# A recurrent attention block with a feed-forward layer: the output product regrouped into four 160-column strips, and the memory rows turned by VectorE instead of TensorE

## The chip, the cores and the metric

The kernel runs on one core of a Trainium2 chip. Its time is the device time of one execution in microseconds (us). Before the change three runs gave a median of 1040.74 us (1040.04 to 1044.46). The engines are TensorE (PE in the profile; its weight loads are shown as PEld), VectorE (DVE), ScalarE (ACT), GpSimd (POOL) and the queue that issues most DMAs (SP).

## The reference

An input of 2048 tokens with 640 channels goes through two layers: `h = x + A(layernorm(x))`, then `h + B(layernorm(h))`. A is attention with 32 heads of 128, computed in 64 segments of 32 tokens, one after the other, because each segment hands 8 memory rows to the next:

```python
mem = mem0                                    # 8 rows of 640
for s in range(64):
    h = concat([mem, x[32*s : 32*s+32]])      # 40 rows
    q, k, v = h @ Wq, h @ Wk, h @ Wv          # 32 heads x 128
    p = softmax(mask(q @ k.T * scale))
    o = (p @ v) @ Wo                          # 40 rows of 640
    mem = o[:8]                               # the next segment needs it
    outs.append(o[8:])
```

B is a feed-forward layer of width 1728 with a squared ReLU. Inputs and outputs are bf16.

## The kernel before

**Stages.** A start-up stage loads the weights and projects the first segment. Then 64 calls of `step` (L368) do one segment each, some 12.9 us apart. At the end the feed-forward layer runs in four tiles of 512 tokens (L780 on).

**What a step does.** The 40 rows of a segment are split: 8 memory rows and the first 24 tokens (the main rows, 32 in all) are handled in the step; the last 8 tokens of four segments are collected to 32 tail rows for whole-block products. TensorE is used in four column groups of 32: four matmuls with weights of 128x32 run side by side and write partitions 0-31, 32-63, 64-95 and 96-127 of one PSUM tile. In this text such four are a round, and a weight load with its matmul is a pair.

The order on TensorE in a step, which is written out by hand and is kept by every engine as written: the projections q, k, q, k from `hT` (`proj`, L194; each 20 pairs of 512 columns), the memory rows' scores, the values' projection v, the scores of the segment's tokens, the attention values of the segment before (`token_values`, L336) and of the memory rows (`values`, L431), then the output product of all 32 heads into the PSUM tile `pw` (`wo_rounds`, L229, called at L542).

**The output product before.** For 16 rounds, the column groups are two halves of the heads (kh) times two halves of the 640 output columns (ch), 320 columns each. So `pw` holds two partial sums in its upper and lower 64 partitions, and `wo_out` (L239) adds them: ScalarE copies the lower half to `otmp` (L243), VectorE adds the upper half to it and writes `o` (L244). The tail rows' product (`wo_tail_units`, L285) works the same way, once for four segments.

**The memory rows' way to the next segment.** `mem_to_hT` (L304) takes `o`, transposes its first rows on TensorE by 20 small matmuls against an identity (L308, tile `pm`), and VectorE copies the result into `hT` (L310), from which the next step's projections read.

**Fill work.** Products that no step waits for are cut into units and put in a list, `fill`: projections of tail rows (units of 4 pairs of 512 columns) or the tail rows' output product (10 units). A step takes one unit at L509, two at L520, five between `wo_out` and `mem_to_hT` (L549) and what is left at L553. `tails_in` (L312) copies the tail rows' q and k into place on GpSimd, and `token_out` (L351) moves attention values on ScalarE and GpSimd. `store_main` (L328) issues the DMAs of finished rows from SP. Five `o` tiles form a ring (`o_ring`).

Of the kernel before, what the change touches and what calls it, by code (L numbers as in the profile page):

```python
# [9 lines left out]
ALU = mybir.AluOpType  # L10
AX = mybir.AxisListType
F32 = mybir.dt.float32
BF16 = mybir.dt.bfloat16
# [3 lines left out]
def kernel(  # L17
# [16 lines left out]
    nc = tc.nc  # L34
    _, S, D = A_x.shape
    _, H, E = A_Wq.shape
    M = A_mem0.shape[1]
    SEG = 32
# [3 lines left out]
    EG = HE // G  # L42
    DC = D // 128
    DH = D // 2
    NB = S // 128
    NS = S // SEG
    HD = 24
# [13 lines left out]
    const = ctx.enter_context(tc.tile_pool(name="const", bufs=1))  # L61
# [6 lines left out]
    s1 = ctx.enter_context(tc.tile_pool(name="s1", bufs=1))  # L68
    s2 = ctx.enter_context(tc.tile_pool(name="s2", bufs=2))

    o_all = dram.tile([S, D], BF16)
# [4 lines left out]
    wo = wts.tile([128, H, D], BF16)  # L76

    ident = const.tile([128, 128], BF16)
# [13 lines left out]
    for g in range(G):  # L92
        r = slice(32 * g, 32 * g + 32)
# [6 lines left out]
    oT = const.tile([128, H, NK], BF16)  # L100
    nc.vector.memset(oT[:], 0.0)
    oTts = [const.tile([128, H, 32], BF16, name="oTt%d" % k) for k in range(2)]
# [3 lines left out]
    def head(p):  # L106

        n, g, j = p // 16, p // 4 % 4, p % 4
        return g * HG + j * 2 + n
# [16 lines left out]
        eng.dma_start(out=xt[:], in_=x2d.rearrange("(s t) d -> s t d", t=SEG)[16 * g:16 * g + 16, HD:SEG, :])  # L126
        xts["t", g] = xt

    o_ring = [const.tile([128, DH], BF16, name="o%d" % k) for k in range(5)]
    for o in o_ring:  # L130
        nc.gpsimd.memset(o[64:128], 0.0)
    o0 = o_ring[-1]
    nc.vector.memset(o0[0:64], 0.0)
    load_x(0)
    for ch in range(2):
        nc.sync.dma_start(out=o0[32 * ch:32 * ch + M, :].rearrange("m (c f) -> m c f", f=64),
                            in_=A_mem0[0].rearrange("m (c t f) -> t m c f", t=2, f=64)[ch])
    load_tail_rows(0)
    load_w(wv, A_Wv)
    def load_wo():  # L140
# [19 lines left out]
    hT4s, hTts, tails = {}, {}, {}  # L160
# [63 lines left out]
    def flip(row, dst, n):  # L224
        nc.vector.transpose(out=dst[:, n * 16:(n + 1) * 16, 0:32], in_=row.rearrange("p (h e) -> p h e", e=32))  # L225

    wov2 = wo[:].rearrange("p h (c t f) -> p h t c f", t=2, f=64)

    def wo_rounds(lhs, pw, h0, h1):  # L229

        for h in range(h0, h1):
            for kh in range(2):
                for ch in range(2):
                    j = kh * 2 + ch
                    p = h // 8 * 16 + kh * 8 + h % 8
                    nc.tensor.matmul(pw[32 * j:32 * j + 32, 0:DH], lhsT=lhs(p), rhs=wov2[:, head(p), ch],  # L236
                                     start=(h == 0), stop=(h == 15))

    def wo_out(pw):  # L239
        o = o_ring[0]  # L240
        o_ring.append(o_ring.pop(0))
        tmp = s1.tile([128, DH], F32, tag="tk", name="otmp")
        nc.scalar.copy(out=tmp[0:64], in_=pw[64:128, 0:DH])  # L243
        nc.vector.tensor_tensor(out=o[0:64], in0=pw[0:64, 0:DH], in1=tmp[0:64], op=ALU.add)  # L244
        return o

    fill, late, mid, win = [], [], [], []

    def run(q, n):
        while n > 0 and q:  # L250
            q.pop(0)()
            n -= 1
# [32 lines left out]
    def wo_tail_units(b):  # L285
        st = {}

        def out():
            o = wo_out(st["ps"])
            dst = o_all[:].rearrange("(b s t) d -> b s t d", s=4, t=SEG)  # L290
            for ch in range(2):
                nc.sync.dma_start(out=dst[b, :, HD:SEG, ch * DH:(ch + 1) * DH], in_=o[32 * ch:32 * ch + 32, :])

        def unit(k):
            def f():
                if k == 0:
                    st["ps"] = mmtile()
                wo_rounds(lambda p: oTts[b % 2][:, p, :], st["ps"], k * 16 // 10, (k + 1) * 16 // 10)
                if k == 9:
                    late.append(out)  # L300
            return f
        return [unit(k) for k in range(10)]

    def mem_to_hT(o, hT4, sp):  # L304
        pm = chn.tile([128, 512], F32, tag="ch", name="pm")
        for c in range(DC):
            for q in range(4):
                nc.tensor.matmul(pm[32 * q:32 * q + 32, c * M:(c + 1) * M], lhsT=o[:, (2 * c + q % 2) * 32:(2 * c + q % 2 + 1) * 32],  # L308
                                 rhs=ident[:, q // 2 * 32:q // 2 * 32 + M], start=True, stop=True)
        nc.vector.tensor_copy(out=hT4[:, :, sp, 0:M], in_=pm[:, 0:DC * M].rearrange("p (c m) -> p c m", m=M))  # L310

    def tails_in(b, sp):  # L312
        q, k = [tails[b][w][:].rearrange("p h (k s) -> p h s k", s=4)[:, :, sp, :] for w in "qk"]
        nc.gpsimd.tensor_copy(out=qT[:, :, SEG:NK], in_=q)
        nc.gpsimd.tensor_copy(out=kT[:, :, SEG:2 * SEG].rearrange("p h (j k) -> p h j k", k=TL),  # L315
                              in_=k.unsqueeze(2).to_broadcast([128, H, 4, TL]))
# [9 lines left out]
            eng.dma_start(out=vt4s[b][32 * g:32 * g + 32].rearrange("p s u e -> p (s u e)"), in_=src[g])  # L326

    def store_main(o, s):  # L328
        for ch in range(2):
            nc.sync.dma_start(out=o_all[s * SEG:s * SEG + HD, ch * DH:(ch + 1) * DH],  # L330
                              in_=o[32 * ch + M:32 * ch + 32, :])

    oTg = oT[:].rearrange("p (n g j) q -> p n g j q", n=2, g=G)
    back = []
# [33 lines left out]
    def step(b, sp, v=None):  # L368
        s = b * 4 + sp
        last = s == NS - 1  # L370
        hT4 = hT4s[b]
        lhs = lambda c: hT4[:, c, sp, :]
# [151 lines left out]
        tk = s1.tile([128, HG, NK], F32, tag="tk", name="tk")  # L524
# [3 lines left out]
        for f in outs:  # L528
# [7 lines left out]
                                op=ALU.mult)  # L536
        pk = s1.tile([128, HG, 32], BF16, tag="pk", name="pk")
        nc.gpsimd.tensor_tensor(out=pk[:], in0=ek[:, :, 0:SEG], in1=rk[:].unsqueeze(2).to_broadcast([128, HG, SEG]),
                                op=ALU.mult)

        pw = chn.tile([128, 512], F32, tag="ch", name="pw")
        wo_rounds(lambda p: oT[:, p, 0:32], pw, 0, 16)  # L542
        o = wo_out(pw)
        if s:
            token_out(s - 1, po)
        if s > 1:
            store_main(o, s - 2)
        if not last:
            run(fill, 5)  # L549
            mem_to_hT(o, hT4s[(s + 1) // 4], (s + 1) % 4)  # L550
            tails_in((s + 1) // 4, (s + 1) % 4)
        run(mid, 2)
        run(fill, 100)  # L553
        pTt = s1.tile([128, 2, 32], BF16, tag="pTt", name="pTt")
# [2 lines left out]
        for u in range(2):  # L557
            nc.gpsimd.tensor_tensor(out=pTx[:, u], in0=pTt[:, u, HD:32].unsqueeze(1).to_broadcast([128, 4, TL]),
                                    in1=same[:], op=ALU.mult)
# [60 lines left out]

    def prep_sum(t, k, got):
        ot, fx = got
        fv = fx.rearrange("p (c t f) -> p t c f", t=2, f=64)
        nc.vector.tensor_tensor(out=fv, in0=ot.rearrange("p (t c f) -> p t c f", t=2, f=64), in1=fv, op=ALU.add)
        return fx

    def prep_norm(t, k, ht, mv, rs):
# [75 lines left out]
    load_w(wq, A_Wq)  # L703
    ln_stats(("t", 0))
    ln_transpose(0)()
    mem_to_hT(o0, hT4s[0], 0)
    ln_norm(("t", 0))
    load_x(1)
    load_w(wk, A_Wk)
# [50 lines left out]

    def end_output(s):
        pw = chn.tile([128, 512], F32, tag="ch", name="pw")
        wo_rounds(lambda p: oT[:, p, 0:32], pw, 0, 16)
        store_main(wo_out(pw), s)

    def end_tails():
# [13 lines left out]
    for t in range(S // NT):  # L780
# [6 lines left out]
        for fc in range(FC):  # L787
            ps = mmtile()
            for c in range(DC):
                if fc < FFULL:  # L790
                    nc.tensor.matmul(ps[:], lhsT=w1[:, c, fc * 128:(fc + 1) * 128], rhs=hnT[:, c, :],  # L791
                                     start=(c == 0), stop=(c == DC - 1))
                    continue
                for hh in range(2):
                    nc.tensor.matmul(ps[FREM * hh:FREM * (hh + 1), 0:HT], lhsT=w1[:, c, fc * 128:F],
                                     rhs=hnT[:, c, HT * hh:HT * (hh + 1)], start=(c == 0), stop=(c == DC - 1))
            w = NT if fc < FFULL else HT
            r = rs_[fc % 4]
            nc.scalar.activation(out=r[:, 0:w], in_=ps[:, 0:w], func=ACT.Relu, bias=b1f[:, fc:fc + 1], scale=1.0)
            nc.vector.tensor_tensor(out=f1T[:, fc, 0:w], in0=r[:, 0:w], in1=r[:, 0:w], op=ALU.mult)  # L800
            if more and fc >= 1 and (fc - 1) // 3 < NK4:
                k, stage = divmod(fc - 1, 3)
# [10 lines left out]
        for q in range(NK4):  # L813
# [6 lines left out]
            for hh in range(2):  # L820
                k = pr + 2 * hh
                for fc in range(FFULL):
                    nc.tensor.matmul(y[:, hh, 0:DH], lhsT=f1T[:, fc, k * 128:(k + 1) * 128], rhs=w2[:, fc, cs],  # L823
                                     start=(fc == 0), stop=False, skip_group_check=True)
                if more and q and (hh == 0 or q == 1):
                    k = q if hh == 0 and q > 1 else hh
# [45 lines left out]
```

## Time and profile before

| what | value |
|---|---|
| median of three runs | 1040.74 us |
| span of the profiled execution, first to last instruction | 1035.5 us |
| from the first to the last step's output product | 66.1 to 881.9 us |
| TensorE busy, pairs | 980.1 us (95%), 26960 |
| VectorE, ScalarE, GpSimd busy | 621.6, 536.0, 312.3 us |
| output product of the main rows (L236, `pw`) | 4224 pairs of 320 columns, 159.6 us |
| output product of the tail rows (L236, `ps`) | 1024 pairs of 320 columns, 47.0 us |
| transposes of the memory rows (L308) | 1280 pairs of 8 columns, 18.6 us |
| granted TensorE clock, mean | 0.993 |

The profiled execution has no total of its own beside its span; the median of the runs lies 5.2 us above the span, which is what lies around it. [...] In the timeline each line gives the start, the length, the engine, the line of code, what is written and read, the shape and the number of merged instructions; in brackets stands how long the engine sat idle before and what ended it. The profile's third part lists DMA queues; the queue called instruction carries the program's own instructions to an engine.

### The profile page before, as it was taken

The page shows a single profiled execution, that of the slowest core. Times are in us where ns is not written, and L with a number is a line of the kernel's source. Part 1 is how long each engine was busy: PE and PEld are TensorE (multiplying, and loading weights), DVE is VectorE, ACT ScalarE, POOL GpSimd, SP SyncE. Part 2 cuts the span into 40 slices and gives each one's busy share as a digit, 9 for nine tenths or more (in the row PEclk, how much of TensorE's full clock was granted, in tenths as well). Part 3 has the DMA queues.
Part 4 walks back from the last instruction along what each step waited for, and adds up shares of the span by engine and source line. Part 5 has one row for each costly group of instructions (what it writes and reads, how often), then busy time and mean ns, then how long its engine had stood idle before and what let it go on. Part 6 is the DMA issues. An engine that isn't in the chain of part 4 may idle for free.

```text
span 1035.5 us, 58905 instructions
## 1 busy us (share of the span) xinstructions
PE 980.1 (95%) x26960; PEld 563.9 (54%) x26960; DVE 621.6 (60%) x1740; ACT 536.0 (52%) x1225; POOL 312.3 (30%) x805
## 2 busy tenths in 40 slices
PE   5879899999999999999999999999999998999998
PEld 2335455555655555555555655555555555555565
DVE  2155666766566666666666666666666676565432
ACT  2435555555555555555555555555555555534431
POOL 1033333333333333332333233333333333343210
PEclk9889999999999999999999999999999999999999
DMA  8960101000100000000000000000000110612200
GB/s 319 405 205 26 22 7 31 7 24 6 32 10 22 15 24 24 16 20 14 26 15 22 15 27 15 22 15 27 15 21 8 47 33 7 194 54 72 77 26 26
DMA packets 39112, 51.58 MB, mean 50 GB/s; under 512 B 6160, under 2 KB 34960, under 8 KB 36944
## 3 DMA queue, kind: packets, MB, share of 16 engines
q1 hardware_dynamic: 38000, 47.30, 13.8%
q8 instruction: 210, 3.44, 1.4%
q14 instruction: 38, 0.31, 0.1%
q10 hardware_dynamic: 544, 0.26, 0.1%
q0 software_dynamic: 320, 0.26, 0.1%
HBM read 38.37 MB, written 9.44 MB: 46 GB/s over the span
## 4 chain that ended last, share of the span: by engine, by line
PE 83%; DMA 6%; DVE 5%; issue 3%; ACT 2%; POOL 0%; SPq 0%; DVEq 0%; ACTq 0%; POOLq 0%
PE ps L204 45%; PE pw L236 13%; PE y L823 6%; PE ps L791 5%; PE ps L236 3%; DMA xt<-in_A_x_dram 3%; PE po L437 2%; PE pm L308 2%; PE sm L409 2%; DMA wq<-in_B_w_dram 1%; PE po L343 1%; PE ps L485 1%; ACT em L418 1%; DMA vt_d<-row 1%; DVE o L244 1%
## 5 line engine op out<-in xcount | busy, mean ns | idle before, releaser
L204 PEld LDWEIGHTS <-hT 128*32 128x32 bf16 x7680 | 186.9, 96 | 180.8 <-DVE hT L310 19.6
L204 PE MATMUL ps<-wv,hT 128*32 128x512 bf16 x2520 | 169.9, 379 | 0.7 <-ACT v L492 0.7
L236 PE MATMUL pw<-wo,oT 128*32 128x320 bf16 x4224 | 159.6, 300 | 3.3 <-DVE pTt L555 1.2
L204 PE MATMUL ps<-wq,hT 128*32 128x512 bf16 x2520 | 158.1, 380 | 4.8 <-DVE hT L310 4.8
L204 PE MATMUL ps<-wk,hT 128*32 128x512 bf16 x2520 | 157.6, 379 | 0.0
L236 PEld LDWEIGHTS <-oT 128*32 128x32 bf16 x4224 | 109.3, 97 | 50.7 <-DVE oT L211 15.8
L535 POOL TENSOR_TENSOR pkt<-ek,rk 128x64 bf16<-128x64 bf16 x64 | 18.8, 294 | 377.6 <-DVE rk L533 377.6
L220 ACT ACTIVATE row<-ps 128x512 bf16<-128x512 f32 x156 | 91.9, 601 | 78.4 <-PE ps L204 74.6
L225 DVE STREAM_TRANSPOSE qT<-row 128x512 bf16<-128x512 bf16 x128 | 90.6, 709 | 51.9 <-ACT row L220 51.9
L222 ACT CAST row<-ps 128x512 bf16<-128x512 f32 x115 | 65.9, 596 | 34.3 <-PE ps L204 34.3
L315 POOL COPY kT<-kTt 128x1024 bf16<-128x1024 bf16 x64 | 70.9, 1108 | 13.7 <-DVE kTt L225 13.7
L362 POOL COPY qz<-qT 128x96 bf16<-128x96 bf16 x126 | 33.4, 265 | 125.0 <-DVE qT L225 121.5
L353 ACT CAST oT<-po 128x512 bf16<-128x512 f32 x128 | 68.7, 589 | 1.6
L244 DVE TENSOR_TENSOR o<-pw,otmp 64x320 bf16<-64x320 f32 x66 | 31.8, 482 | 61.9 <-ACT otmp L243 61.9
L204 PEld LDWEIGHTS <-hTt 128*32 128x32 bf16 x1920 | 48.8, 99 | 35.6 <-issue 9.9
L225 DVE STREAM_TRANSPOSE kT<-row 128x512 bf16<-128x512 bf16 x65 | 46.0, 708 | 31.1 <-ACT row L222 31.1
L243 ACT COPY otmp<-pw 64x320 f32<-64x320 f32 x66 | 27.9, 422 | 70.9 <-PE pw L236 70.9
L823 PE MATMUL y<-wq,wk 128*128 128x320 bf16 x416 | 60.9, 299 | 0.0
L393 ACT CAST row<-ps 128x256 bf16<-128x256 f32 x126 | 40.7, 375 | 29.1 <-PE ps L204 29.0
L531 DVE TENSOR_REDUCE zk<-ek 128x8 f32<-128x320 bf16 x64 | 31.1, 486 | 40.2 <-ACT ek L527 40.2
L527 ACT ACTIVATE ek<-tk 128x320 bf16<-128x320 f32 x64 | 30.1, 470 | 45.1 <-DVE tk L525 45.1
L418 ACT ACTIVATE em<-sm,mx 128x64 bf16<-128x64 f32 x126 | 40.4, 321 | 24.3 <-DVE mx L415 24.3
(114 smaller groups left out, 1657.5 us busy)
## 6 DMA issues: line engine op xcount, KB each, us to landing
wv<-in_A_Wv_dram SPq DMA_DIRECT2D x5, 1024.0 KB
wq<-in_A_Wq_dram SPq DMA_DIRECT2D x5, 1024.0 KB
wk<-in_A_Wk_dram SPq DMA_DIRECT2D x5, 1024.0 KB
wo<-in_A_Wo_dram SPq DMA_DIRECT2D x4, 1280.0 KB
vt<-vt_d SPq DMA_DIRECT2D x60, 64.0 KB
xt<-in_A_x_dram SPq DMA_DIRECT2D x20, 160.0 KB
vt_d<-row SPq DMA_DIRECT2D x22, 128.0 KB
wq<-in_B_w_dram SPq DMA_DIRECT2D x1, 2080.0 KB
```

Of the source, the lines that this page charges most:

```text
L204: nc.tensor.matmul(ps[32 * k:32 * k + 32, :], lhsT=lhs(c), rhs=wr[:, c, n, k], start=(c == 0), stop=(c == DC - 1))
L220: nc.scalar.mul(out=row, in_=ps, mul=scale)
L222: nc.scalar.copy(out=row, in_=ps)
L225: nc.vector.transpose(out=dst[:, n * 16:(n + 1) * 16, 0:32], in_=row.rearrange("p (h e) -> p h e", e=32))
L236: nc.tensor.matmul(pw[32 * j:32 * j + 32, 0:DH], lhsT=lhs(p), rhs=wov2[:, head(p), ch], start=(h == 0), stop=(h == 15))
L244: nc.vector.tensor_tensor(out=o[0:64], in0=pw[0:64, 0:DH], in1=tmp[0:64], op=ALU.add)
L315: nc.gpsimd.tensor_copy(out=kT[:, :, SEG:2 * SEG].rearrange("p h (j k) -> p h j k", k=TL), in_=k.unsqueeze(2).to_broadcast([128, H, 4, TL]))
L353: nc.scalar.copy(out=oTg[:, n, :, :, M:NK], in_=po[:, :, n * 128:(n + 1) * 128].rearrange("p g (j q) -> p g j q", q=32))
L393: nc.scalar.copy(out=row[:, u * 256:(u + 1) * 256], in_=ps[:, u * 256:(u + 1) * 256])
L418: nc.scalar.activation(out=em[:], in_=sms[n][:, 0:2 * SEG], func=ACT.Exp, bias=mx[:, 0:1], scale=1.0, accum_out=zm[:])
L791: nc.tensor.matmul(ps[:], lhsT=w1[:, c, fc * 128:(fc + 1) * 128], rhs=hnT[:, c, :], start=(c == 0), stop=(c == DC - 1))
L823: nc.tensor.matmul(y[:, hh, 0:DH], lhsT=f1T[:, fc, k * 128:(k + 1) * 128], rhs=w2[:, fc, cs], start=(fc == 0), stop=False, skip_group_chec ...
```

## The change

The output product gives each of the four column groups a quarter of the output columns (160) and lets every group sum all 32 heads: 32 rounds of 160 columns in place of 16 of 320. No partial sums are left, so `wo_out` is one ScalarE copy. The columns are dealt out in strips of 32, so that the memory rows can be turned by VectorE's transposes of 32x32 blocks directly from PSUM into `tr`, and a second VectorE instruction copies the 8 rows' columns into `hT`. The 20 small matmuls of each step are gone. In `step`, `mem_to_hT` and `tails_in` now stand ahead of `wo_out` and `token_out`, and the fill units of L549 are no longer called between: all that are left run at the later call. Stores are four DMAs of 160 columns in place of two of 320, and `prep_sum` reads the new column order. The first segment's memory rows are loaded in one DMA and turned by five matmuls.

```diff
-    wov2 = wo[:].rearrange("p h (c t f) -> p h t c f", t=2, f=64)
-    def wo_rounds(lhs, pw, h0, h1):
-        for h in range(h0, h1):
-            for kh in range(2):
-                for ch in range(2):
-                    j = kh * 2 + ch
-                    p = h // 8 * 16 + kh * 8 + h % 8
-                    nc.tensor.matmul(pw[32 * j:32 * j + 32, 0:DH], lhsT=lhs(p), rhs=wov2[:, head(p), ch],
-                                     start=(h == 0), stop=(h == 15))
+    wov4 = wo[:].rearrange("p h (c q f) -> p h q c f", q=4, f=32)
+    def wo_rounds(lhs, pw, p0, p1):
+        for p in range(p0, p1):
+            for q in range(4):
+                nc.tensor.matmul(pw[32 * q:32 * q + 32, 0:DQ], lhsT=lhs(p), rhs=wov4[:, head(p), q],
+                                 start=(p == 0), stop=(p == H - 1))
     def wo_out(pw):
         o = o_ring[0]
         o_ring.append(o_ring.pop(0))
-        tmp = s1.tile([128, DH], F32, tag="tk", name="otmp")
-        nc.scalar.copy(out=tmp[0:64], in_=pw[64:128, 0:DH])
-        nc.vector.tensor_tensor(out=o[0:64], in0=pw[0:64, 0:DH], in1=tmp[0:64], op=ALU.add)
+        nc.scalar.copy(out=o[:], in_=pw[:, 0:DQ])
         return o
...
-                wo_rounds(lambda p: oTts[b % 2][:, p, :], st["ps"], k * 16 // 10, (k + 1) * 16 // 10)
+                wo_rounds(lambda p: oTts[b % 2][:, p, :], st["ps"], k * H // 10, (k + 1) * H // 10)
...
-    def mem_to_hT(o, hT4, sp):
-        pm = chn.tile([128, 512], F32, tag="ch", name="pm")
-        for c in range(DC):
-            for q in range(4):
-                nc.tensor.matmul(pm[32 * q:32 * q + 32, c * M:(c + 1) * M], lhsT=o[:, (2 * c + q % 2) * 32:(2 * c + q % 2 + 1) * 32],
-                                 rhs=ident[:, q // 2 * 32:q // 2 * 32 + M], start=True, stop=True)
-        nc.vector.tensor_copy(out=hT4[:, :, sp, 0:M], in_=pm[:, 0:DC * M].rearrange("p (c m) -> p c m", m=M))
+    def mem_to_hT(pw, hT4, sp):
+        tr = s1.tile([128, DQ], F32, tag="tr", name="tr")
+        nc.vector.transpose(out=tr[:], in_=pw[:, 0:DQ])
+        nc.vector.tensor_copy(out=hT4[:, :, sp, 0:M], in_=tr[:].rearrange("p (c r) -> p c r", r=32)[:, :, 0:M])
...
     def store_main(o, s):
-        for ch in range(2):
-            nc.sync.dma_start(out=o_all[s * SEG:s * SEG + HD, ch * DH:(ch + 1) * DH],
-                              in_=o[32 * ch + M:32 * ch + 32, :])
+        for q in range(4):
+            nc.sync.dma_start(out=o_all[s * SEG:s * SEG + HD, q * DQ:(q + 1) * DQ],
+                              in_=o[32 * q + M:32 * q + 32, :])
...
-        wo_rounds(lambda p: oT[:, p, 0:32], pw, 0, 16)
+        wo_rounds(lambda p: oT[:, p, 0:32], pw, 0, H)
+        if not last:
+            mem_to_hT(pw, hT4s[(s + 1) // 4], (s + 1) % 4)
+            tails_in((s + 1) // 4, (s + 1) % 4)
         o = wo_out(pw)
         if s:
             token_out(s - 1, po)
         if s > 1:
             store_main(o, s - 2)
-        if not last:
-            run(fill, 5)
-            mem_to_hT(o, hT4s[(s + 1) // 4], (s + 1) % 4)
-            tails_in((s + 1) // 4, (s + 1) % 4)
         run(mid, 2)
         run(fill, 100)
```

## The prediction

> **What bounds the kernel now.** I read the first part of the page first.
>
> ```profile
> PE 980.1 (95%) x26960; PEld 563.9 (54%) x26960; DVE 621.6 (60%) x1740; ACT 536.0 (52%) x1225; POOL 312.3 (30%) x805
> ...
> q8 instruction: 210, 3.44, 1.4%
> ```
>
> TensorE is the only engine near its limit. The second line seems idle and decides this forecast: 26960 pairs are 53920 instructions, and 53920/210 = 257, so each packet of queue q8 brings TensorE some 256 instructions, 128 pairs.
>
> Then the timeline of one step, here the end of its output product (first pair at 500.61):
>
> ```profile
> 500.61 2.36 PE L236 MATMUL pw<-wo,oT 128*32 128x320 bf16 x64
> 503.08 0.42 ACT L243 COPY otmp<-pw 64x320 f32<-64x320 f32 x1 [1.03 <-PE pw L236]
> 503.53 0.48 DVE L244 TENSOR_TENSOR o<-pw,otmp 64x320 bf16<-64x320 f32 x1 [0.73 <-ACT otmp L243]
> 504.07 0.29 PE L308 MATMUL pm<-ident,o 128*32 128x8 bf16 x20
> 504.45 0.20 DVE L310 CAST hT<-pm 128x40 bf16<-128x40 f32 x1 [0.43 <-PE pm L308]
> 504.70 1.26 PE L204 MATMUL ps<-wq,hT 128*32 128x512 bf16 x20
> ```
>
> The five short links hand the memory rows on: from the start of the last `pw` matmul (502.67) to the first projection pass 2.03 us. This T is 2.0 to 2.1 us in nearly all of the 63 hand-overs, whatever fill lies inside, so the chain sets it.
>
> Third, the matmul starts around one standstill, and the DMA view of three neighbouring windows (458.4 to 459.4, 459.4 to 461.9, 462.0 to 463.2; only the packet counts are shown):
>
> ```profile
> 459.76 0.62 PE L204 MATMUL ps<-wk,hTt 128*32 128x512 bf16 x8
> 460.25 0.31 PE L236 MATMUL pw<-wo,oT 128*32 128x320 bf16 x1
> 460.91 2.35 PE L236 MATMUL pw<-wo,oT 128*32 128x320 bf16 x63 [0.35 <-issue]
> ```
>
> ```profile
> q8 instruction: 1, 0.02, 5.5%
> ```
>
> ```profile
> DMA packets 1, 0.02 MB, mean 16 GB/s; under 512 B 0, under 2 KB 0, under 8 KB 0
> ```
>
> ```profile
> DMA packets 0, 0.00 MB, mean 0 GB/s; under 512 B 0, under 2 KB 0, under 8 KB 0
> ```
>
> TensorE stops after one pair of the product for 0.66 us, waiting for no engine. A packet started at 458.50, none follows until 462.02. Such stops lie exactly 128 pairs, or multiples of it, apart. Of the 196 borders between the first and last step's product, 31 show over 0.06 us of standstill, 11.2 us together. There TensorE resumes 2.2 to 2.9 us after a packet's start (median 2.6), and the next packet starts a median 1.13 us later. Over all packets the distance of starts is never below 3.32 us, a tenth are below 3.49, the median is 4.07. I read: one block is fetched while the one before runs, never two, so **128 pairs cost at least some 3.5 us**, 27 ns a pair. Before, the loop has 400 pairs a step of 12.95 us, 32 ns a pair; it lives just above that floor.
>
> **The change, part by part.**
>
> *Pace of the new rounds.* By the distance of starts: 16 pairs of 64 columns take 0.11 us (28 ns a round), a round of 320 takes 136.5 ns (2.05 us for 15). On the line between them 160 columns make 69 ns. The product: 32 x 69 = 2.21 us against 16 x 136.5 = 2.18. Reading strips of 32 columns costs nothing: the projections read such strips too, at 216 to 218 ns a round of 512.
>
> [...]
>
> *The hand-over.* Gone: otmp 0.42, add 0.48, 20 transposes, and their hand-offs. New: the last matmul 0.23 (192 ns at 64 columns, 275 at 256), hand-off 0.11 (as 502.97 to 503.08), VectorE transpose, 0.04, copy 0.20 (the L310 row), 0.05. The transpose of 128x160 f32 from PSUM is not in the trace: bf16 rows are 0.245 us for 128x64, 0.424 for 128x256, 0.709 for 128x512; these are the ends, and I take 0.42, the row of nearest size in bytes. Chain: 1.05 us (0.88 to 1.34).
>
> Fill now runs after the product without a break, and T becomes the longer of chain and fill. In 35 hand-overs 28 pairs of fill are left: 7 x 0.216 + 0.07 = 1.58, saving 0.45. In 14 the tail product is left, 92 pairs in the changed order: 23 x 0.069 + 0.07 = 1.66, saving 0.42 of 2.08. In 14 there is little or none: 1.05, saving 0.98. Sum 15.8 + 5.9 + 13.7 = 35.4. The main product's first-to-last start grows from 2.05 to 31 x 0.069 = 2.14, 63 x 0.09 = 5.7; the tail products' early part grows by 14 x 0.075 = 1.1. **Net -28.6 us**, if instructions come in time.
>
> *Refills.* The new order has 458.9 pairs a step in place of 399.7 (64 more in the main product, 16 a step in the tail product, 20 transposes fewer). I cut both orders at every 128 pairs and gave each block its time from the rows: rounds at the paces above (25 ns at 40 columns and fewer: 16 pairs in 0.10 us), plus the waits for other engines as in the timeline, no refill. Then I took what each lacks to 3.5 us:
>
> | | blocks | under 3.5 us | their mean | lacking in all | runs of such |
> |---|---|---|---|---|---|
> | before | 196 | 85 | 2.89 us | 52.2 us | 62 |
> | after | 225 | 139 | 2.55 us | 131.9 us | 62 |
>
> Why: token values, values, the last fill and the product are 152 pairs in 3.5 us before, 216 in the same time after, where 27 ns a pair asks 5.9.
>
> Of the 52.2 only 11.2 show, so 41.0 are covered: what TensorE has already taken in runs on while the next block comes. A run uses that cover up once, and both orders have 62 runs, so I keep 41.0. After: 131.9 - 41.0 = 90.9 us of standstill, **+79.7**. At a floor of 3.4 the same steps give +74, at 3.7 +90.
>
> [...]
>
> *The rest.* ScalarE's copy of `o` now waits for VectorE's transpose in the changed order (0.265 us, the 128x128 row, to 0.42), with `token_out`'s two casts and the fill's row copies queued behind. The next k projection needs the PSUM tile that the first of these frees, about 2.7 us after the last `pw` start, when TensorE wants it at 2.67: 0 to 0.15 us in 35 steps, 0 to 5 us; I take 0, since refills delay TensorE more. VectorE loses 82 adds of 0.48 and gains 63 transposes and is not the bound. SP issues four stores of 0.4 us a step in place of two; it waited 654 us for `o`, which covers that; exposed, the row stores behind them hold a ScalarE copy longer (3.8 us in three cases before): 0 to 3 us. GpSimd's `tails_in` stands ahead of the `oTt` copy, which nothing needs before the next block: 0. Start and end: the first segment's load and the feed-forward layer wait for weight DMAs (13.4 and 15.0 us in the chain): 0.
>
> Sum: -28.6 + 79.7 = +51. The span is 1035.5 us, the median of the runs 1040.7, 5.2 around it; 1040.7 + 51 = **1092 us**.
>
> **The rivals.**
>
> *Refills stay hidden* (faster). The place is the block border. If more than one block could lie ready, the supply only had to hold on average, and the price is nil: 1040.7 - 28.6 = 1012 us. It decides from packets under 3.3 us apart. Against it: not one pair of packets came so close, though blocks as short as 2.3 us were there. [...]
>
> *The cover grows.* If it belongs to each short block and not to each run (41.0/85 = 0.48 us), 139 x 0.48 = 67 are covered, standstill 65, +54 - 28.6: 1066 us. For it: I inferred the cover and measured only its sum.
>
> *Another engine takes the gain.* ScalarE's backlog after the product (copy, casts, two row copies, 2.5 us) delays the q copy, the flips and the scores; with refills hidden, the 35 x 0.45 are lost: 1028 us; with them it hides behind the standstill.
>
> **How the numbers follow.** Forecast 0.72, refills hidden 0.10, cover grows 0.14, another engine with hidden refills 0.04. The forecast spreads from 1070 to 1112 (floor 3.4 to 3.7 with the costs taken as 0; the short end if part of the standstill falls into waits that are there anyway). With the third case the range is 1060 to 1112. A measurement can tell about 0.5%, 5 us, from no change. Faster 0.13, the same 0.02, slower 0.85.
>
> **What would show it.** Right: q8 with about 242 packets, most distances 3.4 to 3.8 us; `issue` ahead of L230 (the new `pw` line) and of the values; some 90 us of standstill at borders of 128 pairs; T of 1.1 to 1.7 us where no border falls; rounds of 69 ns. Wrong: packets under 3.3 us apart, or TensorE idle before the first projection behind `tr`, or rounds of 100 ns within a block.

## The result, and the profile after

The changed kernel takes 1112.77 us (four runs, 1111.35 to 1114.71); the kernel before, now over four runs, 1042.29 (1040.04 to 1044.46). The ratio is 1.068, with a 95% interval of 1.066 to 1.070. The forecast was 1092 in a range of 1060 to 1112: the direction and the cause held, the size was 21 us too small, and the time lies 0.8 us above the upper end.

The page of the changed kernel, its first, third and fourth parts:

```profile
PE 983.0 (89%) x30933; PEld 664.3 (60%) x30933; DVE 637.2 (57%) x1721; ACT 520.9 (47%) x1225; POOL 306.2 (28%) x800
...
q8 instruction: 241, 3.95, 1.5%
...
PE 80%; issue 9%; DMA 5%; DVE 4%; ACT 1%; POOL 0%; SPq 0%; DVEq 0%; ACTq 0%; POOLq 0%
```

TensorE is busy for about the same 980 us as before, in a span 75 us longer. It has 30933 pairs in place of 26960, and the instruction queue brings 241 packets in place of 210 (30933 x 2 / 241 = 257 instructions each, as before). In the chain, "issue" went from 3% to 9%: time in which TensorE waited for no other engine. The chain and the product's wait of the kernel before, for comparison:

```profile
PE 83%; DMA 6%; DVE 5%; issue 3%; ACT 2%; POOL 0%; SPq 0%; DVEq 0%; ACTq 0%; POOLq 0%
```

```profile
PE pw L236 <- issue: 0.9, 3, 0.3
```

The view of TensorE's waits in the changed kernel says where (total us, times, longest):

```profile
PE pw L230 <- issue: 50.4, 61, 2.8
PE ps L230 <- issue: 16.9, 15, 1.6
PE ps L201 <- DVE hT L299: 10.7, 12, 1.5
...
PE ps L201 <- issue: 7.7, 13, 1.2
...
PE po L433 <- issue: 4.7, 12, 0.7
```

The new product (L230) is where it stops. The third line, a wait for the memory rows behind L299, was not expected; it comes back below. TensorE's timeline of one step with a tail product:

```profile
277.30 0.60 PE L230 MATMUL ps<-wo,oTt 128*32 128x160 bf16 x24
277.73 0.73 PE L230 MATMUL pw<-wo,oT 128*32 128x160 bf16 x32
279.52 1.84 PE L230 MATMUL pw<-wo,oT 128*32 128x160 bf16 x96 [1.07 <-issue]
281.18 0.74 PE L230 MATMUL ps<-wo,oTt 128*32 128x160 bf16 x32
283.26 1.22 PE L230 MATMUL ps<-wo,oTt 128*32 128x160 bf16 x60 [1.34 <-issue]
284.29 1.27 PE L201 MATMUL ps<-wq,hT 128*32 128x512 bf16 x20
```

The number behind the x counts pairs. From one stop to the next there are 96 + 32 = 128. Their work takes from 279.52 to 281.92 (283.26 less 1.34), 2.4 us, and then TensorE stands for 1.34 us. Packets of the instruction queue start at 276.91, 280.65 and 284.42; TensorE goes on 2.61 us after each of the first two. One block, one packet, one stop: this is the picture of the forecast, at twice the depth of the stop that it showed (0.66 us).

Counted at every border of 128 pairs between the first and the last step's product (standstill over 0.06 us), there are now 116 stops of 102.1 us in all, in place of 31 of 11.2 us; the largest groups are 75 in the product (77.7 us), 19 in the projections (13.4), 16 in the values (7.5).

### The profile page after: what moved, and what is told of

It is laid out like the page before. It is cut to its first block, busy times and chain, and to the rows that moved or that the text cites. A ratio compares the mean times of both kernels' runs of the same rounds, so it can differ in the third digit from the quotient of the medians.

```text
span 1110.6 us, 67292 instructions
## 1 busy us (share of the span) xinstructions
PE 983.0 (89%) x30933; PEld 664.3 (60%) x30933; DVE 637.2 (57%) x1721; ACT 520.9 (47%) x1225; POOL 306.2 (28%) x800
## 4 chain that ended last, share of the span: by engine, by line
PE 80%; issue 9%; DMA 5%; DVE 4%; ACT 1%; POOL 0%; SPq 0%; DVEq 0%; ACTq 0%; POOLq 0%
PE ps L201 43%; PE pw L230 15%; PE y L818 5%; PE ps L786 5%; PE ps L230 4%; DMA xt<-in_A_x_dram 3%; PE po L433 2%; PE sm L405 2%; PE po L339 1%; PE ps L481 1%; DVE hT L299 1%; DMA wq<-in_B_b_dram 1%; ACT em L414 1%; DMA vt<-vt_d 1%; PE pt L176 1%
## 5 line engine op out<-in xcount | busy, mean ns | idle before, releaser
L201 PEld LDWEIGHTS <-hT 128*32 128x32 bf16 x7680 | 231.6, 96 | 156.6 <-DVE hT L299 20.0
L230 PE MATMUL pw<-wo,oT 128*32 128x160 bf16 x8448 | 175.1, 235 | 52.4 <-issue 50.4
L230 PEld LDWEIGHTS <-oT 128*32 128x32 bf16 x8448 | 151.2, 98 | 80.3 <-issue 61.9
L201 PE MATMUL ps<-wq,hT 128*32 128x512 bf16 x2520 | 168.0, 381 | 12.3 <-DVE hT L299 10.7
L201 PE MATMUL ps<-wv,hT 128*32 128x512 bf16 x2520 | 175.2, 381 | 0.7 <-ACT v L488 0.7
L201 PE MATMUL ps<-wk,hT 128*32 128x512 bf16 x2520 | 166.9, 380 | 0.0
L236 ACT CAST o<-pw 128x160 bf16<-128x160 f32 x66 | 19.3, 293 | 155.0 <-DVE tr L298 142.8
L201 PEld LDWEIGHTS <-hTt 128*32 128x32 bf16 x1920 | 56.7, 99 | 41.0 <-issue 15.4
L311 POOL COPY kT<-kTt 128x1024 bf16<-128x1024 bf16 x64 | 71.2, 1113 | 12.5 <-DVE kTt L222 12.5
L298 DVE STREAM_TRANSPOSE tr<-pw 128x160 f32<-128x160 f32 x63 | 22.0, 350 | 82.0 <-PE pw L230 82.0
L230 PE MATMUL ps<-wo,oTt 128*32 128x160 bf16 x2048 | 48.0, 233 | 16.9 <-issue 16.9
```

The source lines that it names most:

```text
L201: nc.tensor.matmul(ps[32 * k:32 * k + 32, :], lhsT=lhs(c), rhs=wr[:, c, n, k], start=(c == 0), stop=(c == DC - 1))
L230: nc.tensor.matmul(pw[32 * q:32 * q + 32, 0:DQ], lhsT=lhs(p), rhs=wov4[:, head(p), q], start=(p == 0), stop=(p == H - 1))
```

## The experiments

The **theory**: TensorE's instructions arrive in blocks of 128 pairs, one ahead, and a block costs at least 3.5 us or a little more; the change packs more pairs into the same work. The **rivals**: the new rounds or the new order are slow by themselves; or the new hand-over (copies, stores, ScalarE's queue) is. Standstill in the experiments is counted by another rule, the same for all: TensorE goes on 2.1 to 3.1 us after a packet's start. By it the kernel before has 14.2 us, the changed one 98.5.

**A row of tiny pairs, nothing else.** The kernel before, with 1280 pairs of 8 columns put into the feed-forward layer.

```diff
+        if t == 1:
+            pr = chn.tile([128, 512], F32, tag="ch", name="probe")
+            for i in range(320):
+                for q in range(4):
+                    nc.tensor.matmul(pr[32 * q:32 * q + 32, 0:8], lhsT=ident[:, 0:32], rhs=ident[:, 0:8],
+                                     start=True, stop=True, skip_group_check=True)
         for fc in range(FC):
```

> The kernel before, with 1280 additional pairs of 8 columns (25 ns a round of four by the rows for 8 to 40 columns) in one go ahead of the second tile of the feed-forward layer. Theory (instructions come to TensorE in blocks of 128 pairs, one block fetched while the one before runs): the 1280 pairs are 10 blocks and take 10 x 3.5 = 35 us, 27 ns a pair, with stops of about 2.5 us every 128 pairs and packets of q8 some 3.5 us apart; the time goes up by about 34 us to some 1075 us. Rival (small matmuls cost only their own pace, and the stops had another cause): 1280 x 6.3 to 8.3 ns = 8 to 11 us, time about 1052 us, no stops.

It took 1079.76 us in its one run, 38 more than before and 5 more than the theory's 1075; the rival's 1052 is out. Its timeline, TensorE alone:

```profile
943.10 2.03 PE L791 MATMUL probe<-ident 128*32 128x8 bf16 x230
948.00 1.19 PE L791 MATMUL probe<-ident 128*32 128x8 bf16 x128 [2.87 <-issue]
952.57 1.19 PE L791 MATMUL probe<-ident 128*32 128x8 bf16 x128 [3.38 <-issue]
956.58 1.19 PE L791 MATMUL probe<-ident 128*32 128x8 bf16 x128 [2.83 <-issue]
960.05 1.19 PE L791 MATMUL probe<-ident 128*32 128x8 bf16 x128 [2.28 <-issue]
963.80 1.19 PE L791 MATMUL probe<-ident 128*32 128x8 bf16 x128 [2.56 <-issue]
967.27 1.19 PE L791 MATMUL probe<-ident 128*32 128x8 bf16 x128 [2.28 <-issue]
971.29 1.19 PE L791 MATMUL probe<-ident 128*32 128x8 bf16 x128 [2.83 <-issue]
974.76 1.19 PE L791 MATMUL probe<-ident 128*32 128x8 bf16 x128 [2.28 <-issue]
```

This is the mechanism alone: the first 230 pairs lay ready, then each run is of exactly 128, done in 1.0 us (8 ns a pair), and TensorE stands. The starts are 4.57, 4.01, 3.47, 3.75, 3.47, 4.02 and 3.47 us apart: **3.47 at best, 3.82 in the mean**. The forecast took 3.5 for all. The mean of a row without any cover is 0.3 us more. From 948 us on the granted clock of this row is 0.50, though, so by itself this run can't say whether the lower clock lengthens the blocks; the part on the prediction answers that from the changed kernel's loop.

**More pairs, no other change.** The kernel before, with 64 pairs of 8 columns ahead of each step's product, as many as the change adds to it.

```diff
         pw = chn.tile([128, 512], F32, tag="ch", name="pw")
+        for i in range(16):
+            for q in range(4):
+                nc.tensor.matmul(pw[32 * q:32 * q + 32, 320:328], lhsT=ident[:, 0:32], rhs=ident[:, 0:8],
+                                 start=True, stop=True, skip_group_check=True)
         wo_rounds(lambda p: oT[:, p, 0:32], pw, 0, 16)
```

> The kernel before, with 64 additional pairs of 8 columns ahead of each step's output product, written to columns of the PSUM tile that nobody reads. It has the number of pairs of the changed kernel (464 a step against 459), but its product has 320 columns and its hand-over is the old one. Theory (refills): own pace 64 x 64 x 6.3 ns = 25 us, and by the block table 120 us lack to 3.5 us a block in place of 52, of which 30 to 41 are covered: standstill 79 to 90 us in place of 11. Time 1042 + 25 + 68 to 79 = 1135 to 1146 us. Rival (the narrow rounds of the output product are what costs): only the own pace, 1067 to 1076 us.

1158.59 us in its one run, 117 more, above the theory's range and far from the rival's. The loop, from the first to the last step's product, grew by 114 us (815.8 to 930.0); 75.6 of that is counted standstill (14.2 to 89.8). The old product, unchanged, now waits for instructions, and so do the added pairs (L544):

```profile
PE pw L236 <- issue: 38.8, 34, 2.0
PE pw L544 <- issue: 24.7, 29, 3.0
```

So the added pairs alone bring nearly the change's standstill (75.6 us more, against 84.3), with the old product, the old transposes and the old stores.

Their own work is an estimated 25 us (63 x 16 rounds of 25 ns). What is left of the 114, some 13 us, fits something that the forecast did not have at all. In ten stretches of 3.4 us in this loop, 34 us in all, the granted clock is 0.50. First the product that lies in one of them, then the clock there (the third number from the end is the granted clock):

```profile
305.42 4.04 PE L236 MATMUL pw<-wo,oT 128*32 128x320 bf16 x64
```

```profile
305.90:309.10 3.20, 3.20 (x56) 2.44 (x52) 0.10 (x1) 0.00 (x0) 0.87 (x2) 0.50 0.02 5
```

The same 64 pairs take 2.36 us at the full clock. Half of 34 us is 17, and a part of it falls into standstill, so 13 fits. The kernel before has no such stretch in its loop, the changed one has two (118 and 183 us). Each of the ten begins in a stop of over 1 us or within 1.2 us of its end; that the stops bring them about was not tried, and many stops as long have none.

**Fewer pairs.** The changed kernel, with the tail product (not the main one) in halves as before: 64 pairs of 320 columns in place of 128 of 160, with the old sum on ScalarE and VectorE and two stores.

```diff
...
-                wo_rounds(lambda p: oTts[b % 2][:, p, :], st["ps"], k * H // 10, (k + 1) * H // 10)
+                tail_rounds(lambda p: oTts[b % 2][:, p, :], st["ps"], k * 16 // 10, (k + 1) * 16 // 10)
```

> The changed kernel, with the tail rows' product alone put back to two halves of the heads of 320 columns (64 pairs in place of 128, with the sum on ScalarE and VectorE): 443.7 pairs a step in place of 458.9. Theory (refills): 110 us lack in the block table in place of 132, so some 21 us less standstill: about 1092 us (1087 to 1098), and the stops inside the tail product, 2.8 to 3.2 us of hand-over in each fourth step, become short. Rival (the stops belong to the main product and the new hand-over): the tail product's own pace is the same to 0.02 us, so the time stays within 1108 to 1115 us.

1096.53 us (1095.36 to 1097.30), ratio to before 1.053 (1.051 to 1.055): 16 us better than the changed kernel, standstill 84.8 in place of 98.5. That lies in the theory's range (1087 to 1098), and the rival's (1108 to 1115) is out.

**Narrower rounds, as many pairs.** The changed kernel, with 96 columns in place of 160 in all rounds but the first; it leaves out the other columns' share of 31 heads.

```diff
-                nc.tensor.matmul(pw[32 * q:32 * q + 32, 0:DQ], lhsT=lhs(p), rhs=wov4[:, head(p), q],
+                cs = DC if p == 0 else 3
+                nc.tensor.matmul(pw[32 * q:32 * q + 32, 0:32 * cs], lhsT=lhs(p), rhs=wov4[:, head(p), q, 0:cs],
```

> The changed kernel, with all pairs of the output products kept, but all rounds except the first of a product cut from 160 to 96 columns: two fifths of the output columns get the first head's share alone. Theory (refills): the column time falls by 31 x 27 ns x 82 = 69 us, of which little is seen, because the pairs come no faster: the lack rises from 132 to 177 us. Time 1113 less 5 to 20: 1093 to 1108 us. Rival (the product costs by its columns and rounds): 55 to 70 us less, 1043 to 1058 us.

1116.91 us (1112.65 to 1124.66), ratio 1.074 (1.068 to 1.079): above the theory's 1093 to 1108 too, and far from the rival's 1043 to 1058. Some 69 us of TensorE's work are gone (82 products x 31 rounds x 27 ns, an estimate) and not one is gained: the standstill grew by 50, from 98.5 to 148.5 us. Most of the rest fits the clock: 34 us of this loop have a granted clock of 0.50 (7 in the changed kernel), which is up to 14 us more. The waits for instructions in the product (L231 here) took what the work gave back:

```profile
PE pw L231 <- issue: 82.0, 62, 3.4
PE ps L231 <- issue: 28.2, 15, 2.5
```

The rival, slow rounds, falls with this: what a round costs here is mostly its four pairs' share of a block.

**The shorter hand-over, with no pair added.** The kernel before; ScalarE copies both halves of `pw` to bf16, the 20 transposes add the halves with weights of two ones, and the add for the store follows later on GpSimd and VectorE.

```diff
...
-                                 rhs=ident[:, q // 2 * 32:q // 2 * 32 + M], start=True, stop=True)
+                                 rhs=pick[:, q // 2, :], start=True, stop=True)
...
-        o = wo_out(pw)
+        ob = both(pw)
...
+        if not last:
+            run(fill, 4)
+            mem_to_hT(ob, hT4s[(s + 1) // 4], (s + 1) % 4)
+        o = add_halves(ob)
...
```

> The kernel before, with its product of two halves, but the memory rows leave by a shorter chain: ScalarE copies both halves of `pw` to bf16, the 20 small matmuls sum the two halves while they transpose (their weights hold a one for each half), and the add on VectorE (0.48 us) is done later, for the store alone. No pair is added to TensorE's program. Theory (the hand-over is on the path, and only the added pairs ate its gain): the time from the last `pw` start to the first projection falls from 2.03 to some 1.55 to 1.8 us, a part of it goes to more standstill at block borders since the loop gets denser; 13 to 25 us faster than before, 1016 to 1028 us. Rival (the hand-over is not what the loop waits for; the supply of instructions is the limit already before): 0 to 5 us, 1036 to 1041 us.

1048.94 us (1047.19 to 1050.07), ratio 1.0075 (1.005 to 1.010): **slower than before** by some 0.8%, outside both. The first half of the theory held: T, from the last `pw` start to the first projection, fell from 2.03 to 1.76 in 34 steps, from 2.08 to 1.88 in 14 and from 2.03 to 1.52 in 12, 19.4 us in all. But the stretch from the first projection to the scores grew by 20.5 us (270.6 to 291.1 over 62 steps, median 4.36 to 4.53). Two lines of this kernel's page name the new wait:

```profile
L331 POOL COPY kT<-kTt 128x1024 bf16<-128x1024 bf16 x64 | 72.4, 1131 | 12.5 <-DVE kTt L229 12.5
...
L260 DVE TENSOR_TENSOR o<-ob,o 64x320 bf16<-64x320 bf16 x64 | 20.3, 318 | 80.4 <-POOL o L259 38.3
```

The add on VectorE (L260) stands 80 us idle, 38 of them for GpSimd's new copy (L259, 0.45 us each), and VectorE's transposes of q and k, which the scores need, stand in its queue behind the add. So q and k are turned later (in one such step `qT` starts 3.6 us after the first projection, 1.9 before), and `qz` and the scores with them. The gain was real and was given back one stretch later.

**Fewer transposes, wider.** The same, with 10 transposes of 64-column weights.

```diff
-            for q in range(4):
-                nc.tensor.matmul(pm[32 * q:32 * q + 32, c * M:(c + 1) * M], lhsT=o[:, (2 * c + q % 2) * 32:(2 * c + q % 2 + 1) * 32],
-                                 rhs=pick[:, q // 2, :], start=True, stop=True)
+            for ch in range(2):
+                nc.tensor.matmul(pm[64 * ch:64 * ch + 64, c * M:(c + 1) * M], lhsT=o[:, c * 64:(c + 1) * 64],
+                                 rhs=pick[:, ch, :], start=True, stop=True)
```

> As v1_sum_in_transpose, with the 20 transposes of 32 columns replaced by 10 with weights of 64 columns: 10 pairs a step fewer, 640 in all, 5 blocks of 128. Theory (each block border has a price where blocks are short): 1 to 6 us faster than v1_sum_in_transpose. Rival (fewer pairs are worth nothing, or the change between 32 and 64 columns costs more than it gains): equal or slower.

1050.95 us (1045.96 to 1051.74), ratio 1.008 (1.006 to 1.011): not better than its sibling, and by the spread of the two not clearly worse; the rival holds. Five packets fewer came (205), but T in the 34 common steps rose from 1.76 to 2.00 us. In the medians of these steps the way into the transposes (from the last start before) grew from 205 to 309 ns, the transposes themselves from 114 to 151, the way back to fill from 15 to 102: 0.23 us, nearly all of the difference, for going from 32 to 64 columns and back.

**GpSimd's copies back in their place.** The changed kernel, with `tails_in` behind `token_out` as before.

```diff
             mem_to_hT(pw, hT4s[(s + 1) // 4], (s + 1) % 4)
-            tails_in((s + 1) // 4, (s + 1) % 4)
...
+        if not last:
+            tails_in((s + 1) // 4, (s + 1) % 4)
```

> The changed kernel with the call of `tails_in` (GpSimd's copies of the tail rows' q and k) put back behind `token_out`, as before the change; nothing else differs. In the changed kernel the VectorE copy hT<-tr takes 0.59 us in the mean (0.18 to 1.12), where 0.20 was expected. Theory (GpSimd's copies, which now start with the product's end, hold up VectorE's copy): the copy falls to 0.2 to 0.3 us, and since most of its wait lies beside fill and standstill, the whole gains 3 to 10 us, 1103 to 1110 us. Rival (the copy of f32 rows with a stride is slow by itself): it stays near 0.59 us and the time at 1113 within 3 us.

First a hand-over of the changed kernel as it was, the timeline of three engines:

```profile
469.54 1.09 POOL L311 COPY kT<-kTt 128x1024 bf16<-128x1024 bf16 x1
469.56 0.35 DVE L298 STREAM_TRANSPOSE tr<-pw 128x160 f32<-128x160 f32 x1 [1.34 <-PE pw L230]
...
469.95 0.72 DVE L299 CAST hT<-tr 128x40 bf16<-128x40 f32 x1
...
470.73 4.01 PEld L201 LDWEIGHTS <-hT 128*32 128x32 bf16 x80 [1.27 <-DVE hT L299]
470.73 1.26 PE L201 MATMUL ps<-wq,hT 128*32 128x512 bf16 x20 [0.78 <-DVE hT L299]
```

VectorE's copy L299 ends (470.67) when GpSimd's copy of `kT` does (470.63), and TensorE waits for it. The same copy in the two kernels, changed first, `tails_in` put back second (min/median/max, ns):

```profile
L299 DVE CAST hT<-tr x63: 182/579/1117, 68.7 to 955.5; 128x40 bf16<-128x40 f32 x63
```

```profile
L299 DVE CAST hT<-tr x63: 182/183/256, 68.5 to 954.3; 128x40 bf16<-128x40 f32 x63
```

That settles it: the copy is 0.18 us, and up to 1.12 while GpSimd copies from SBUF to SBUF; the transpose from PSUM just ahead of it takes 349 to 352 ns in all 63 cases, 62 of them beside GpSimd's work. In all 51 hand-overs in which the copy took over 0.26 us, it ended 35 to 45 ns after an instruction of GpSimd did; the longest, 1117 ns, began 30 ns after GpSimd's `kT` copy (1113 ns in the mean). So in these the copy ended just behind an instruction of GpSimd; what makes it wait there, no run shows. T in the 12 steps with little fill fell from 1.34 and 1.49 to 0.90 us, and TensorE's wait behind the copy from 10.7 to 5.5 us. The whole moved less: 1108.47 us, ratio to before 1.064 (1.061 to 1.068) against 1.068 (1.066 to 1.070). That is 4 us, in the theory's range, but with intervals that overlap, so a gain of the whole is not shown.

**Fill spread through the product.** The changed kernel, with up to four fill units between the product's rounds.

```diff
-        wo_rounds(lambda p: oT[:, p, 0:32], pw, 0, H)
+        for k in range(8):
+            wo_rounds(lambda p: oT[:, p, 0:32], pw, 4 * k, 4 * k + 4)
+            if k % 2 == 0:
+                run(fill, 1)
```

> The changed kernel with up to four fill units (of 4 pairs of 512 columns, or a tenth of the tail product) spread between the rounds of the output product, in place of behind it. The pairs are the same in number; the short rounds of 69 ns are mixed with rounds of 216 ns. Theory (what counts is how much TensorE time each 128 pairs hold; the product and the fill together stay the same number of pairs in the same time): the stops in the product shrink a little, but the fill no longer covers the memory rows' way, some 0.9 us in up to 49 steps; 1100 to 1130 us, no gain of over 15 us. Rival (the stops come from the product's own rhythm, such as its writing one PSUM tile, and not from blocks of 128 pairs): they fall by half or more, and the time to under 1095 us.

1115.81 us (1114.33 to 1117.70), ratio 1.072 (1.069 to 1.075), as the theory had it. The standstill fell only from 98.5 to 92.0, and the projections' wait for the memory rows rose from 10.7 to 15.2 us. The order of dense and thin rounds within a step hardly matters.

**The change's hand-over with no more pairs than before.** The changed kernel in everything, but both products in 16 rounds of 320 columns; it leaves out half of the heads.

```diff
-        for p in range(p0, p1):
+        for p in range(p0 + p0 % 2, p1, 2):
             for q in range(4):
-                nc.tensor.matmul(pw[32 * q:32 * q + 32, 0:DQ], lhsT=lhs(p), rhs=wov4[:, head(p), q],
-                                 start=(p == 0), stop=(p == H - 1))
+                nc.tensor.matmul(pw[32 * q:32 * q + 32, 0:DH], lhsT=lhs(p), rhs=wov4[:, head(p), q // 2 * 2:q // 2 * 2 + 2],
+                                 start=(p == 0), stop=(p == H - 2))
```

> The changed kernel with its VectorE transposes, stores and order, but both output products in 16 rounds of 320 columns, as many pairs and as much TensorE time as before; it leaves out half of the heads from the products. Without the 20 transposes a step it has 379 pairs a step, fewer than the 399.7 before. Theory (the new hand-over is worth what it was worked out to be, and only the added pairs cost): standstill of 5 to 15 us, 18 to 30 us faster than before, 1011 to 1023 us. Rival 1 (the hand-over's gain goes into later waits of the step, as in v1_sum_in_transpose): 1035 to 1045 us. Rival 2 (a part of the loss in the changed kernel comes from elsewhere than the pairs: the four stores, ScalarE's longer queue, the copies): 1045 us or more.

1012.93 us (1010.28 to 1014.01), ratio 0.975 (0.973 to 0.977): 25 us faster than before, in the theory's range, both rivals out. Its hand-over in the timeline:

```profile
502.71 2.36 PE L230 MATMUL pw<-wo,oT 128*32 128x320 bf16 x64
...
504.89 1.68 PE L201 MATMUL ps<-wk,hTt 128*32 128x512 bf16 x28
...
505.12 0.35 DVE L298 STREAM_TRANSPOSE tr<-pw 128x160 f32<-128x160 f32 x1 [0.22 <-PE pw L230]
...
505.50 0.45 DVE L299 CAST hT<-tr 128x40 bf16<-128x40 f32 x1
...
506.40 1.25 PE L201 MATMUL ps<-wq,hT 128*32 128x512 bf16 x20
```

The memory rows are ready at 505.95, and the fill ends at 506.40: here TensorE waits for nobody, as the forecast had it for 35 steps. T is 1.64 us in 34 steps and 1.62 in 14; over all hand-overs it falls by 32.6 us (129.4 to 96.8). The counted standstill rises by 6 (14.2 to 20.4): a denser loop meets the floor more often. The stretch from the first projection to the next product grew by 12 us over 62 steps (556.4 to 568.7), of which that standstill is at most half; what holds the rest was not looked into. So the four stores, the longer ScalarE queue and the new copies can have cost at most some 12 us here, and not the changed kernel's 70.

**The shorter hand-over without GpSimd.** As the kernel that came out at 1048.94, but VectorE adds the halves behind its copy of the memory rows, and the small matmuls write free columns of `pw`.

```diff
...
-        nc.gpsimd.tensor_copy(out=o[0:64], in_=ob[64:128])
-        nc.vector.tensor_tensor(out=o[0:64], in0=ob[0:64], in1=o[0:64], op=ALU.add)
+        nc.vector.tensor_tensor(out=o[0:64], in0=pw[0:64, 0:DH], in1=ob[64:128], op=ALU.add)
...
-        pm = chn.tile([128, 512], F32, tag="ch", name="pm")
+        pm = pw[:, DH:512] if pw is not None else chn.tile([128, 512], F32, tag="ch", name="pm")
```

> As v1_sum_in_transpose, but GpSimd has no part in the add: VectorE adds the upper half from the bf16 copy to the lower half in PSUM, behind its copy of the memory rows, and the small matmuls write free columns of `pw`. In v1_sum_in_transpose the way from the last `pw` start to the first projection fell by 0.27 to 0.50 us in each step (19.4 us in all), and the stretch from there to the next product grew by 25 us, most of it in waits on GpSimd's qz and kT. Theory (GpSimd's added copy of 0.45 us delayed these): that stretch falls back to near 554 us, and the time is 12 to 25 us below before, 1016 to 1029 us. Rival (a shorter hand-over by itself moves the wait to the scores): the stretch stays at 570 us or more, 1036 to 1050 us.

**1026.20 us** (1022.86 to 1027.75), ratio 0.987 (0.985 to 0.989): it beats both kernels and computes the whole. T is as in its sibling (1.76, 1.88, 1.58), the stretch from the first projection to the scores is back to 274.2 us, and the one from there to the next product stayed near its sibling's (288.5 against 290.0). Both together are 562.7 us in 62 steps, between the theory's 554 and the rival's 570, where the sibling has 581.2. So GpSimd's copy, with VectorE's wait for it, had taken most of the gain. The small matmuls also moved into `pw` here; what that alone does was not tried.

## Why the prediction was right in kind and short in size

The profiled span grew by 75.1 us (1035.5 to 1110.6), where the sum had +51. The terms, with what the traces give for each:

| term | forecast | measured | from |
|---|---|---|---|
| standstill at block borders | +79.7 | +90.9 | 102.1 - 11.2 |
| hand-over and pace of the rounds | -28.6 | -22.7 | what remains: loop +70.5, less the rows above and below |
| one step early in the loop | 0 | +2.3 | see below |
| start and end | 0 | +4.6 | span +75.1, less loop +70.5 |

**The step that failed is the size of the refill term: the floor of 3.5 us for every block.** 3.5 is near the lower edge of what was seen before (a tenth of the distances were below 3.49), where few blocks followed each other short. In the changed kernel short blocks are the rule, and the row of tiny pairs, nothing but such blocks, shows 3.82 us in the mean, 3.47 at best. The forecast's own sentence, "at 3.7 +90", is what was measured: 11 of the 24 missing us are this term's. The other three experiments with more pairs lean the same way: by the same tables at 3.5 us less 41.0 of cover, 78.7, 69.5 and 135.6 us of standstill would be left for the 64 extra pairs, the tail product in halves and the narrow rounds; 89.8, 84.8 and 148.5 were counted, 11 to 15 more each. These sums can't tell a higher floor from a smaller cover. The changed kernel's own loop can. In it 49 blocks of 128 pairs both begin and end at a gap of over 0.3 us between starts for which no engine is named, so nothing covers them. From one resumption to the next they take 3.45 to 3.48 us (22 times), 3.73 to 3.76 (20) or 4.00 to 4.03 (7), **3.66 in the mean**, all at the full clock. In the kernel before, no block of the loop begins and ends so. Between the forecast's two sums, 3.66 gives an estimate of +88. So it was the floor that was too low, and the cover of 41.0 held well enough.

**That blocks are not hidden and lie only one ahead**: right. Each run of the tiny pairs is one block, and none came sooner than 3.47 us. In the changed loop no packet starts less than 3.33 us after the one before; the median is 3.76, and 119 of 223 distances lie in the forecast's 3.4 to 3.8. For matmuls of 8 columns in four groups that run shows 1.0 us of issue for a block against 3.47 and more from one block to the next.

**The pace of the rounds**: right. 31 rounds of 160 columns take 2.164 us from first to last start where their border brings no stop, 69.8 ns each (69 forecast).

**The hand-over**: the mechanism is right (the run with no more pairs gained 25 us), its size in the changed kernel up to 6 us short. That -22.7 is a remainder: it also holds the two stretches of half the clock, 6.8 us long, an estimated 3.4 us of loss that the forecast did not have. The transpose was dearer in the estimate than on the chip (0.42 against 0.350), the copy cheaper (0.20 against 0.59 in the mean). The copy's row was right; that `tails_in`, moved ahead, would hold it up was not seen: GpSimd's move was looked at for who waits for its results, and not for what VectorE does meanwhile. T without a stop is 1.51 in the steps with 28 fill pairs and 1.60 with the tail product (1.58 and 1.66 forecast); in the steps with little fill it is 1.3 to 1.5 in place of 1.05, and 0.90 with the copies put back. One of the forecast's own signs of being wrong, TensorE idle before the first projection behind `tr`, did appear: the 12 waits of 10.7 us behind L299.

**"SP four stores: 0 to 3 us"**: once, in an early step, the bias load for the feed-forward layer stood in SP's queue behind the four stores; GpSimd's copy of it waited 5.17 us (2.45 before), and TensorE 2.82 for `qz` behind it (0.55 before). This is read from the trace and was not tried by itself. So are the 4.6 us at the ends: the end grew by 5.6, where the chain goes through a load of the second layer's bias and the granted clock is 0.50 for 6.8 us (968 to 975), and the start fell by 1.

**The rivals**: refills hidden, a cover that grows with each short block (1066), and another engine taking the gain are all out by the standstill's size; the last is what befell the first version of the shorter hand-over instead.

The sum was also set on a median 5.2 us above the profiled span, while the changed kernel's own profiled execution took 1112.39, 1.8 us above its span, and its median lies 2.2 above: 3 of the missing 24 us came back there (75.1 - 3.1 = 72.0 = 1112.8 - 1040.7).

## What to carry to other kernels

Divide TensorE's span by its pairs before you trade wide matmuls for more narrow ones: here rows of blocks below some 27 to 30 ns a pair (3.47 to 3.82 us for 128 pairs) ran at the pace of the instruction queue, and neither less work per pair (1116.91 us against 1112.77) nor another order (1115.81) helped. Look at the granted clock of such a stretch as well. When work is moved to a new place, ask of each queue not only who waits for it but which engine it now runs beside. A gain on one hand-over is worth what the next wait leaves of it, so look at the stretch behind it as well: the same shortcut gave +8 us with GpSimd's copy in one add and -12 without it.

## What the runs showed that was not expected

- Blocks of instructions in a row come 3.47, 3.75 or about 4.02 us apart, once 4.57: in steps, not evenly spread. The same steps show at the full clock (changed loop, 3.66 in the mean) and at half of it (tiny pairs, 3.82).
- Some loops with many long stops also lost clock: 34 us at 0.50 with the 64 tiny pairs a step and with the narrow rounds, 7 us in the changed kernel, none before.
- VectorE's small copy from SBUF went from 0.18 to as much as 1.12 us beside GpSimd's copies, while its transpose from PSUM beside the same copies stayed within 3 ns (349 to 352).
- Going from 32-column weights to 64 and back cost some 0.23 us a step, more than the ten pairs it saved.
